# Windowed attention and an ELU layer on one core: queries and keys of batches 1 (second half), 2 and 3 loaded as token blocks and transposed by DMA

## The chip, the core and the metric

The kernel runs on one core of a Trainium2 chip. The metric is the device time of one execution in microseconds; a lower time is better. Engines are named as in the profile: PE is TensorE (PEld its weight load), DVE is VectorE, ACT is ScalarE, POOL is GpSimd and SP is SyncE. SP, ACT and POOL issue DMAs; the data are moved by sixteen DMA engines that all queues share.

## The reference, cut to what matters

```python
# q, k, v: [8 batches, 8 heads, 576 tokens, 64] float32
scores = q @ k.T / 8                      # per batch and head
scores = where(|i - j| <= 32, scores, -1e9)
attn   = softmax(scores)
x      = (attn @ v), heads side by side    # [4608 tokens, 512]
h      = x @ w_in                          # w_in  [512, 2048]
g      = where(h > 0, h, exp(min(h, 0)) - 1)
out    = g @ w_out                         # w_out [2048, 512], out float32
```

The window is narrow: a block of 64 queries needs the 128 keys around it and no others.

## The kernel before

Everything is computed in bf16 with float32 sums. The order of the instructions on every engine is written out by hand; nothing reorders it.

**The layer.** The 4608 tokens are 18 tiles of 256. A tile goes through 8 steps; in each step two blocks of 128 hidden columns are made (`mm1`, L734), ACT takes the exponential (L744), DVE subtracts one (`subtract`, L756; for steps 1, 3 and 4 ACT does it, L754), DVE takes maximum and minimum (`elu`, L767), and two steps later `mm2` adds the product with w_out (L787). There are 144 steps; the first 16 interleave tiles 0 and 1. `elu` of a step runs on DVE at the start of the next one, ahead of the slot "dve".

**Attention beside it.** The queries are 36 pairs of blocks of 64 (`pair i` is blocks 2i and 2i+1; nine blocks are a batch). A table `begin` gives the step at which a pair's `scores` run; from pair 6 on, two pairs begin in one step: pairs 6 and 7 in step 18, 8 and 9 in 26, 10 and 11 in 31, 12 and 13 in 37, then two in every eighth step. One step later comes `mask`, two later `pv` (the product with V), three later `normalize`. The result x must be transposed to xT, [features, tokens], which `mm1` reads: two pairs make a tile. Up to pair 9 TensorE does that (`x_transpose`); from pair 10 on a DMA on SP's queue does (`x_dma`, L455), in steps begin + 3 and begin + 4. Tile 5 is made of pairs 10 and 11, and its first step is step 40.

**Slots.** `at(step, slot, function)` notes work; `run` issues it in the slots "first", "dve" (before `mm1`), "half" (in the middle of it), "mid" (after it) and "end". So where an entry stands decides its place in the queue of its engine, and an engine that waits holds up all that stands behind it.

**Queries and keys.** Scores need qT and kT, [head dimension, tokens], two buffers each for even and odd batches. The data come as float32 with tokens outside. Before the change there are three ways:

- Batches 0 and 1, first half: cast and transposed in pieces at the front.
- Batch 1, second half (`HALF_B`), and batch 2: loaded as float32 on SP (`load_qk`, L132, in pieces of 9 or 18 tokens of one head, 2,304 or 4,608 bytes each), cast to bf16 by ACT or DVE (`cast_qk`, L290, L292), transposed by TensorE in groups of nine (`transpose_qk`, L340) and copied from PSUM by ACT. A one-element DMA, `gate`, holds these loads on SP until the weights are there.
- Batches 3 to 7: loaded and cast in the same way, then written to DRAM by ACT's queue (`write_rows`, L319) and brought back transposed by a DMA on SP (`transpose_rows`, L324).

**V.** `load_v` (L151) loads blocks of 128 tokens of V on POOL's queue, with a cast, into one of three buffers V_e. Blocks with an odd index need V shifted by 64 rows, V_o: it is copied on DVE (`rotate_v`, L175) or by two DMAs on SP (`rotate_v_dma`, L183). `hold_v` is a tiny DVE instruction that makes the loads of a batch wait for a step.

The output rows leave on SP (L803), two stores of 256 KB for a tile.

Of the kernel before, what the change touches and what calls it, by code (L numbers as in the profile page):

```python
# [10 lines left out]
BF16 = mybir.dt.bfloat16  # L11
# [10 lines left out]
def kernel(  # L22
# [9 lines left out]
    nc = tc.nc  # L32

    B, H, S, D = q.shape
# [9 lines left out]
    HP = H // 2  # L44
    NC = 128 // HP
    SJ = S // NC
    VS = 5
# [15 lines left out]
    lpool = ctx.enter_context(tc.tile_pool(name="loads", bufs=2))  # L63
# [53 lines left out]
    HJ = SJ // 2  # L117
    WHOLE, HALF_A, HALF_B = (0, SJ), (0, HJ), (NC * HJ, HJ)
# [4 lines left out]
    def load_qk(b, which, part, engs=(nc.sync, nc.sync)):  # L123
        z, nj = part
        mj = max(nj, HJ)
        t = lpool.tile([128, 2, mj * D], FP32, tag=f"f{which}{mj}",
                       name=f"f{which}", bufs=2 if part is WHOLE else 1)
        qk_f[b, which, z] = t
        src = (q, k)[which][b, :, z:z + NC * nj, :].rearrange(
            "(g h) (c j) d -> c g h (j d)", h=2, j=nj)  # L130
        for h in range(2):
            engs[h].dma_start(out=t[:, h, 0:nj * D], in_=src[:, :, h, :])  # L132
# [4 lines left out]
    def load_cast(b, which, part):  # L137
        z, nj = part
        mj = nj if nj < 3 else HJ + 1
        t = cpool.tile([128, 2, mj * D], BF16, tag=f"c{which}{mj}",  # L140
                       name=f"c{which}")[:, :, 0:nj * D]
        qk_c[b, which, z] = t
        src = (q, k)[which][b, :, z:z + NC * nj, :].rearrange(
            "(g h) (c j) d -> c g h (j d)", h=2, j=nj)
        nc.gpsimd.dma_start(out=t, in_=src)

    def load_v(b, m, rows=(0, 128)):
        lo = 128 * m - WIN
        p0 = max(rows[0], -lo)
        p1 = min(rows[1], S - lo)  # L150
        nc.gpsimd.dma_start(  # L151
            out=V_e[b % 3][p0:p1, m, :, 0:D],
            in_=v[b, :, lo + p0:lo + p1, :].rearrange("h p d -> p h d"))
# [37 lines left out]
    def gate(src, dt=BF16, eng=nc.sync):  # L191
        gates[0] += 1
        t = cpool.tile([1, 1], dt, name=f"gate{gates[0]}")
        eng.dma_start(out=t, in_=src)

    def load_w_in(c, z=0, nz=1):
        w = D_FF // 4 // nz
        c = c * nz + z
        nc.gpsimd.dma_start(
            out=w_in_sb[:, :, c * w:(c + 1) * w],  # L200
            in_=moe_w_in[:, c * w:(c + 1) * w].rearrange(
                "(o p) f -> p o f", p=128))

    def load_w_out(c, z=0, nz=1):
        n = NFO // 4 // nz
        c = c * nz + z
        nc.gpsimd.dma_start(
            out=w_out_sb[:, c * n:(c + 1) * n, :],
            in_=moe_w_out[c * n * 128:(c + 1) * n * 128, :].rearrange(
                "(o p) f -> p o f", p=128))  # L210

    def w_in_at(c):
        return w_in_sb[0:1, 0, (c + 1) * (D_FF // 4) - 1:(c + 1) * (D_FF // 4)]

    for which in range(2):
        load_qk(0, which, HALF_A, (nc.sync, nc.scalar))
# [4 lines left out]
    def edges(i):  # L221
# [24 lines left out]
        out=far, in_=far, compare_op=ALU.is_ge, fill=FAR,  # L246
        base=0, pattern=[[0, 2], [-1, QB]], channel_multiplier=1)
    nc.gpsimd.affine_select(
        out=far, in_=far, compare_op=ALU.is_ge, fill=FAR,
        base=2 * WIN, pattern=[[0, 2], [1, QB]], channel_multiplier=-1)  # L250
    nc.gpsimd.affine_select(
        out=far[:, 0, :], in_=far[:, 0, :], compare_op=ALU.is_ge, fill=FAR,
# [55 lines left out]
    def keys_or_queries(b, which):  # L308
        if which == 0:
            return qT[b % 2].rearrange("p g s -> p (g s)")  # L310
        return kT[b % 2][:, KPAD:KPAD + HP * S]
# [146 lines left out]
    def first_pair(b):  # L458
        return NQB * b // 2
# [27 lines left out]
    for which in range(2):  # L487
        load_cast(0, which, FRONT_B[which])
# [9 lines left out]
    for which in range(2):  # L498
        load_cast(0, which, FRONT_C[which])
# [4 lines left out]
    BOTH = (nc.scalar, nc.vector)  # L504
# [42 lines left out]
    for which in range(2):  # L547
        load_cast(1, which, HALF_A)
# [3 lines left out]
        load_v(1, m)  # L552
    load_w_in(3)
    load_w_out(3)
    for m in range(3, VS):
        load_v(1, m)
    gate(w_in_at(3))
    for which in range(2):
        load_qk(1, which, HALF_B)
    for which in range(2):  # L560
        load_qk(2, which, WHOLE)

# [3 lines left out]
    def at(kk, slot, fn, *args):  # L568
        tasks.setdefault((kk, slot), []).append((fn, args))
# [34 lines left out]
    for which in range(2):  # L604
        at(8 + which, (6, "half")[which], transpose_qk, 1, which, HALF_A, 0,
           HJ, nc.scalar, "s")
        at(14 + which, "mid", cast_qk, 1, which, HALF_B, 0, HJ, BOTH[which])
        at(15 + which, "end", transpose_qk, 1, which, HALF_B, 0, HJ,
           nc.scalar, "s")
    at(6, "dve", edges, 2)  # L610
    at(16, "dve", hold_v, 2)
    for m in range(VS):
        at(16 + m, "mid", load_v, 2, m)
    at(12, "dve", rotate_v, 1, 0, 2)
    for z in range(2):
        at(14 + z, "dve", rotate_v, 1, 2, VS - 1, (z,))

# [4 lines left out]
    for i in range(4, NPAIR):  # L624
        two = i >= FIRST_TWO
        kk, z = begin[i], i % 2 if two else 0
# [5 lines left out]
        n = kk + (3 + z if two else 2)  # L632
# [11 lines left out]
    for b in range(2, B):  # L644
        k0 = begin[first_pair(b)]


        l_qk, l_v, c0 = {2: (0, 0, 0), 3: (15, 24, 22), 4: (35, 36, 41),
                         5: (52, 52, 57), 6: (68, 68, 73),
                         7: (84, 84, 89)}[b]  # L650
        if b >= 3:
            at(l_qk, "end", load_qk, b, 0, WHOLE)
            at(l_qk, "end", load_qk, b, 1, WHOLE)
            if b > 3:
                at(l_v, "dve", hold_v, b)
            for m in range(VS):
                at(l_v + m, "mid", load_v, b, m)
        if b <= 3:

            if b == 2:  # L660
                at(k0, "dve", rotate_v, b, 0, 1)
            at((21, 28)[b - 2], "mid", rotate_v_dma, b, 3 - b)
        else:
            for n, back in enumerate((10, 8, 3, 2)):
                m0 = 2 * (n // 2)
                at(k0 - back, "dve", rotate_v, b, m0, m0 + 2, (n % 2,))
        if b == 2:

            for n, (which, j0) in enumerate(((0, 0), (0, 9), (1, 0), (1, 9))):
                at((18, 20, 21, 23)[n], ("mid", "end", "end", "mid")[n],  # L670
                   cast_qk, b, which, WHOLE, j0, 9,
                   (nc.vector, nc.scalar, nc.scalar, nc.vector)[n])
                at(22 + n, "end" if n == 1 else "mid", transpose_qk, b, which, WHOLE, j0, 9,
                   nc.scalar, "su"[n % 2])
            continue


        free = [f for f in range(c0, k0) if f not in starts]
        for n, (which, j0) in enumerate(
                (which, j0) for which in range(2) for j0 in (0, 6, 12)):  # L680
            at(free[n], "end", cast_qk, b, which, WHOLE, j0, 6,
               nc.vector if free[n] < 26 else nc.scalar)
            if j0 == 12:
                at(free[n], "end", write_rows, b, which)
                at(free[n] + (3 if free[n] == 29 else 4), "mid",
                   transpose_rows, b, which)

# [50 lines left out]
    def exponents(kk, z):  # L740
        ps = psH[kk][z]
        e_sb = mpool.tile([128, ps.shape[1], TT], FP32, tag="e_sb",
                          name="e_sb")
        nc.scalar.activation(e_sb, ps, AX.Exp)  # L744
        e_t[kk, z] = e_sb
        if kk > 0:
            subtract(kk, z)

    def subtract(kk, z):
        e_sb = e_t.pop((kk, z))  # L750
        m_sb = mpool.tile([128, e_sb.shape[1], TT], BF16, tag="m_sb",
                          name="m_sb")
        if kk in (1, 3, 4):
            nc.scalar.activation(m_sb, e_sb, AX.Copy, bias=-1.0)  # L754
        else:
            nc.vector.tensor_scalar(m_sb, e_sb, -1.0, None, ALU.add)  # L756
        m_t[kk, z] = m_sb

    def elu(kk, z=0):
        if z == 0:  # L760
            g_t[kk] = mpool.tile([128, FG, TT], BF16, tag="g_sb", name="g_sb",
                                   bufs=8)
        if kk == 0:
            subtract(kk, z)
        ps = psH[kk][z]
        w = ps.shape[1]
        nc.vector.scalar_tensor_tensor(  # L767
            g_t[kk][:, z * w:(z + 1) * w, :], ps, 0.0, m_t.pop((kk, z)),
            ALU.max, ALU.min)
# [119 lines left out]
```

## Time and profile before

| | |
|---|---|
| median of 3 runs | 302.76 us (302.54 to 302.93) |
| the profiled execution | 302.52 us, its span 300.8 us |
| PE busy, transposes L340 included | 291.8 us, 97% |
| DVE, ACT, POOL busy | 240.9, 170.2, 52.7 us |
| transposes of q and k, L340 | 72, of them 54 between 43 and 93 us (4.0 us busy) |
| queue q1 (SP): packets, MB | 47330, 35.61 |
| queue q0 (POOL): packets, MB | 44976, 10.10 |
| first product of steps 18, 26, 31, 37, 40 | 51.96, 69.92, 80.66, 92.57, 99.19 us |

The times in the profile count from the start of the span; 1.7 us of the execution lie around it. Busy shares are averages over the whole span. A DMA row has the issue time on its queue and, apart from it, the time to landing. q0 is the queue of POOL, q1 that of SP, q10 that of ACT. A packet is one piece of one transfer; its size is counted at the destination, so a row of 64 elements is 128 bytes.

### The profile page before, as it was taken

Reading aid. Unit: us, or ns where it says so; the run is one execution under the profiler, and the core shown is the slowest. Engines: PE = TensorE matmul, PEld = TensorE weight load, DVE = VectorE, ACT = ScalarE, POOL = GpSimd, SP = SyncE. Lnnn points to the kernel's source line nnn. Section 1 sums busy time; section 2 is a strip of 40 time slices with the busy share of each in tenths; the row PEclk is TensorE's granted clock in tenths of the full one; section 3 lists DMA queues with packets and bytes.
Section 4 is the critical chain, followed back from the end, with each engine's and each line's share of the span. In section 5 each row is a group of like instructions: output and inputs, shape, how many; then the busy total and the mean of one; then the engine's idle time right before and its main releaser. Section 6 shows DMA issues by size and latency. Waiting matters only on the chain.

```text
span 300.8 us, 7664 instructions
## 1 busy us (share of the span) xinstructions
PE 291.8 (97%) x3066; PEld 198.6 (66%) x3118; DVE 240.9 (80%) x479; ACT 170.2 (57%) x258; POOL 52.7 (18%) x74
## 2 busy tenths in 40 slices
PE   7899999999999999999999999999999999999995
PEld 3585567677666666666666666666666666666673
DVE  7788588978787988888889789887988787877773
ACT  3783648688655567456745665467535353534342
POOL 8777203520005000410032002300000000000000
PEclk9999999999999999999999999999999999999999
DMA  9999999999957978999899989997921111111011
GB/s 190 168 200 203 185 233 349 370 179 231 241 159 199 239 116 270 244 267 135 161 256 323 172 203 252 312 153 137 268 54 72 35 72 38 70 37 70 2 70 71
DMA packets 94070, 52.68 MB, mean 175 GB/s; under 512 B 78163, under 2 KB 83795, under 8 KB 94035
## 3 DMA queue, kind: packets, MB, share of 16 engines
q1 hardware_dynamic: 47330, 35.61, 44.7%
q0 software_dynamic: 44976, 10.10, 44.2%
q10 hardware_dynamic: 1728, 6.49, 6.3%
q8 instruction: 24, 0.39, 0.6%
q14 instruction: 12, 0.09, 0.1%
HBM read 36.70 MB, written 15.34 MB: 173 GB/s over the span
## 4 chain that ended last, share of the span: by engine, by line
PE 85%; DMA 5%; issue 3%; DVE 2%; ACT 2%; POOL 2%; POOLq 0%; ACTq 0%; DVEq 0%
PE ps L734 39%; PE psY L787 38%; PE psS L416 4%; DMA out_dram<-y_sb 3%; PE psS L384 3%; DMA c<-in_k_dram 2%; ACT e_sb L744 1%; DVE g_sb L767 1%; PE ptx L335 1%; PE psXT L438 1%; POOL Vo L158 1%; DVE qkb L292 0%; ACT qkb L290 0%; PE ptx L340 0%; PE psS L364 0%
## 5 line engine op out<-in xcount | busy, mean ns | idle before, releaser
L744 ACT ACTIVATE e_sb<-ps 128x512 f32<-128x512 f32 (+1 forms) x145 | 86.3, 596 | 113.4 <-PE ps L734 106.0
L734 PE MATMUL ps<-xT,w_in_sb 128*128 128x256 bf16 (+1 forms) x1168 | 149.7, 271 | 0.1
L787 PE MATMUL psY<-w_out_sb,g_sb 128*128 128x512 bf16 (+2 forms) x541 | 139.3, 373 | 2.9 <-issue 0.3
L734 PEld LDWEIGHTS <-w_in_sb 128*128 128x128 bf16 x1168 | 110.4, 98 | 36.8 <-issue 0.8
L767 DVE SCALAR_TENSOR_TENSOR g_sb<-ps,m_sb 128x512 bf16<-128x512 f32 (+1 forms) x145 | 99.3, 686 | 13.1 <-DVE m_sb L756 0.5
L756 DVE TENSOR_SCALAR m_sb<-e_sb 128x512 bf16<-128x512 f32 (+1 forms) x142 | 61.5, 433 | 34.3 <-ACT e_sb L744 32.3
L787 PEld LDWEIGHTS <-g_sb 128*128 128x128 bf16 x592 | 55.9, 98 | 38.7
L151 POOL DMA_DIRECT2D Ve<-in_v_dram x37 | 32.5, 892 | 132.8 <-PE psS L416 79.5
L395 ACT ACTIVATE pu<-psS 128x1024 bf16<-128x1024 f32 x36 | 36.6, 1023 | 0.9 <-PE psS L384 0.8
L428 DVE TENSOR_TENSOR x_st<-psS,rc 128x512 bf16<-128x512 f32 x36 | 24.9, 692 | 1.2
L290 ACT CAST qkb<-f 128x768 bf16<-128x768 f32 (+1 forms) x29 | 25.0, 862 | 0.0
L404 DVE TENSOR_TENSOR pm<-pu,masks 128x1024 bf16<-128x1024 bf16 x32 | 21.8, 682 | 0.0
L416 PEld LDWEIGHTS <-pm 128*64 128x64 bf16 x512 | 9.6, 110 | 7.3 <-DVE pm L404 6.5
L292 DVE COPY y_sb<-psY 128x512 f32<-128x512 f32 (+1 forms) x18 | 12.2, 676 | 1.5 <-PE psY L787 1.5
L384 PEld LDWEIGHTS <-kT 64*128 64x128 bf16 x560 | 9.4, 95 | 4.6 <-issue 4.4
L290 ACT COPY y_sb<-psY 128x512 f32<-128x512 f32 (+1 forms) x19 | 10.8, 569 | 2.5 <-PE psY L787 2.5
L384 PE MATMUL psS<-qT,kT 64*128 64x64 bf16 x560 | 11.8, 191 | 0.1
L416 PE MATMUL psS<-Ve,pm 128*64 128x65 bf16 x288 | 11.5, 196 | 0.1
L290 ACT COPY qT<-ptx 128x1152 bf16<-128x1152 bf16 (+4 forms) x9 | 7.7, 882 | 5.0 <-PE ptx L340 3.5
L416 PE MATMUL psS<-Vo,pm 128*64 128x65 bf16 x224 | 10.3, 196 | 0.0
L175 DVE COPY Vo<-Ve 64x1040 bf16<-64x1040 bf16 (+1 forms) x22 | 9.1, 413 | 0.7
L425 DVE RECIPROCAL rc<-psS 128x8 f32<-128x8 f32 x36 | 7.2, 199 | 0.9 <-PE psS L416 0.9
(54 smaller groups left out, 91.3 us busy)
## 6 DMA issues: line engine op xcount, KB each, us to landing
out_dram<-y_sb SPq DMA_DIRECT2D x36, 256.0 KB, 3.5
f<-in_q_dram SPq DMA_DIRECT2D x12, 576.0 KB, 6.3
f<-in_k_dram SPq DMA_DIRECT2D x12, 576.0 KB, 8.0
in_dram<-qkb ACTq DMA_DIRECT2D x10, 576.0 KB, 4.2
Ve<-in_v_dram POOLq DMA_DIRECT2D x21, 128.0 KB, 12.6
w_out_sb<-in_moe_w_out_dram POOLq DMA_DIRECT2D x3, 512.0 KB, 10.4
Ve<-in_v_dram POOLq DMA_DIRECT2D x14, 96.0 KB, 11.6
w_in_sb<-in_moe_w_in_dram POOLq DMA_DIRECT2D x2, 512.0 KB, 10.4
```

The costliest lines, as they stand in the source:

```text
L151: nc.gpsimd.dma_start(out=V_e[b % 3][p0:p1, m, :, 0:D], in_=v[b, :, lo + p0:lo + p1, :].rearrange("h p d -> p h d"))
L290: nc.scalar.copy(d_, s_)
L384: nc.tensor.matmul(psS[:, h % 2, hp * 128 + z * QB:hp * 128 + (z + 1) * QB], lhsT=keys, rhs=qT[b % 2][base:base + 64, hp, QB * qb:QB * (qb ...
L395: nc.scalar.activation(pu, _bap(psS, [psS.ap[0], [1, 1024]]), AX.Exp, scale=SCALE)
L404: nc.vector.tensor_mul(pm, pu, _bap(mm, [mm.ap[0], [0, H], [1, 2 * QB]]))
L416: nc.tensor.matmul(psS[QB * z:QB * (z + 1), par, hp * VD:(hp + 1) * VD], lhsT=pm[:, par * HP + hp, z * QB:(z + 1) * QB], rhs=vv[:, qb // 2 ...
L428: nc.vector.tensor_mul(x_st, _bap(psS, [psS.ap[0], [VD, HP], [512, 2], [1, D]]), _bap(rc, [rc.ap[0], [2, HP], [1, 2], [0, D]]))
L734: nc.tensor.matmul(o, lhsT=w_in_sb[:, do, fo * 128:(fo + 1) * 128], rhs=r, start=(do == 0), stop=(do == NDO - 1))
L744: nc.scalar.activation(e_sb, ps, AX.Exp)
L756: nc.vector.tensor_scalar(m_sb, e_sb, -1.0, None, ALU.add)
L767: nc.vector.scalar_tensor_tensor(g_t[kk][:, z * w:(z + 1) * w, :], ps, 0.0, m_t.pop((kk, z)), ALU.max, ALU.min)
L787: nc.tensor.matmul(sum_of(t, ts, c), lhsT=g_t[n][:, j, ts * 128:(ts + 1) * 128], rhs=w_out_sb[:, s * FG + j, cols_of(c)], start=(s == 0 an ...
```

## The change

Queries and keys of the second half of batch 1, of batch 2 and of batch 3 take a new way. `load_tokens` loads a block of up to 128 tokens of all heads on POOL's queue, with the cast, into a bf16 tile [tokens, 512], in runs of 64 elements. `transpose_tokens` is a DMA on SP that writes the block transposed into qT or kT. Batch 1 has six blocks of 96 tokens, batches 2 and 3 ten each (four of 128 and one of 64, for q and for k). The blocks of batch 1 are put on POOL's queue after the last weights and ahead of the last two V blocks of batch 1; those of batch 2 follow, then V of batch 2, the blocks of batch 3 and V of batch 3. The casts, TensorE's transposes and the copies from PSUM of these parts go, and so do batch 3's way through DRAM, the gate, the early `hold_v` and one of the two buffers for float32 loads. `rotate_v` of batch 1 moves from steps 14 and 15 to 17 and 18, `rotate_v_dma` of batches 2 and 3 from steps 21 and 28 to 23 and 33. In the odd steps from 17 to 31 the subtraction goes from DVE to ACT.

```diff
-                       name=f"f{which}", bufs=2 if part is WHOLE else 1)
+                       name=f"f{which}", bufs=1)
...
+    def load_tokens(b, which, s0, n):
+        tag = f"tok{which}{s0}" + ("h" if b == 1 else "")
+        t = lpool.tile([128, H * D], BF16, tag=tag, name="tok", bufs=1)
+        tokens[b, which, s0] = t, n
+        nc.gpsimd.dma_start(
+            out=t[0:n].rearrange("p (h d) -> p h d", h=H),
+            in_=(q, k)[which][b, :, s0:s0 + n, :].rearrange("h p d -> p h d"))
+
+    def transpose_tokens(b, which, s0):
+        t, n = tokens.pop((b, which, s0))
+        nc.sync.dma_start_transpose(
+            out=keys_or_queries(b, which).rearrange(
+                "x (g s) -> x g s", g=HP)[:, :, s0:s0 + n],
+            in_=t[0:n])
...
+    REST = [(s0, 96) for s0 in range(NC * HJ, S, 96)]
+    BLOCKS = [(s0, min(128, S - s0)) for s0 in range(0, S, 128)]
+    rest = [(which, *blk) for blk in REST for which in range(2)]
+    blocks = sorted(((which, *blk) for blk in BLOCKS for which in range(2)),
+                    key=lambda x: (x[1] - x[0] * 129, x[0]))
+    for x in rest:
+        load_tokens(1, *x)
     for m in range(3, VS):
         load_v(1, m)
-    gate(w_in_at(3))
-    for which in range(2):
-        load_qk(1, which, HALF_B)
-    for which in range(2):
-        load_qk(2, which, WHOLE)
+    for x in blocks:
+        load_tokens(2, *x)
...
-        at(14 + which, "mid", cast_qk, 1, which, HALF_B, 0, HJ, BOTH[which])
-        at(15 + which, "end", transpose_qk, 1, which, HALF_B, 0, HJ,
-           nc.scalar, "s")
...
-    at(16, "dve", hold_v, 2)
     for m in range(VS):
-        at(16 + m, "mid", load_v, 2, m)
+        at(12, "mid", load_v, 2, m)
     at(12, "dve", rotate_v, 1, 0, 2)
     for z in range(2):
-        at(14 + z, "dve", rotate_v, 1, 2, VS - 1, (z,))
+        at(17 + z, "dve", rotate_v, 1, 2, VS - 1, (z,))
+    for which, s0, n in rest:
+        at(14, "end", transpose_tokens, 1, which, s0)
+    for which, s0, n in blocks:
+        at(18, "end", transpose_tokens, 2, which, s0)
+        at(19, "mid", load_tokens, 3, which, s0, n)
+        at(30, "mid", transpose_tokens, 3, which, s0)
+    for m in range(VS):
+        at(20, "mid", load_v, 3, m)
...
-            at((21, 28)[b - 2], "mid", rotate_v_dma, b, 3 - b)
+            at((23, 33)[b - 2], "mid", rotate_v_dma, b, 3 - b)
...
-        if kk in (1, 3, 4):
+        if kk in (1, 3, 4) or kk in range(17, 32, 2):
             nc.scalar.activation(m_sb, e_sb, AX.Copy, bias=-1.0)
```

The loads, casts, groups of transposes and the way through DRAM of batches 2 and 3 go from the loop over batches, which now begins these at batch 4.

## The prediction

> **What bounds the kernel now.** I read the page's busy shares first, then its slices, then the groups of instructions and the timeline between 43 and 110 us, where the change acts, and last the DMA queues window by window.
>
> ```profile
> PE 291.8 (97%) x3066; PEld 198.6 (66%) x3118; DVE 240.9 (80%) x479; ACT 170.2 (57%) x258; POOL 52.7 (18%) x74
> ...
> DMA  9999999999957978999899989997921111111011
> ```
>
> TensorE is busy 97% of the span, so time comes off only where TensorE gets less work, and goes on wherever it must wait. The DMA row is the warning: from the start to about 83 us the sixteen DMA engines are full, and from 90 to 218 us (slices of 7.5 us) they are at seven tenths or more. The timeline of TensorE shows what a step costs (one line for each step's first product):
>
> ```profile
> 65.41 1.04 PE L734 MATMUL ps<-xT,w_in_sb 128*128 128x256 bf16 x8
> 66.28 0.67 PE L340 MATMUL ptx<-ident,qkb 128*128 128x128 bf16 x9
> ...
> 67.68 1.03 PE L734 MATMUL ps<-xT,w_in_sb 128*128 128x256 bf16 x8
> ...
> 72.35 1.04 PE L734 MATMUL ps<-xT,w_in_sb 128*128 128x256 bf16 x8
> ...
> 74.09 1.04 PE L734 MATMUL ps<-xT,w_in_sb 128*128 128x256 bf16 x8
> ```
>
> Step 24 (65.41) lasts 2.27 us, with nine transposes in it; step 27 (72.35), with nothing extra, 1.74. So nine transposes are worth about 0.5 us of the path, less than their 0.67 busy, since they are pipelined.
>
> **What the skill says.** "DMA: Bandwidth & Descriptors", "Queues, rings and completion order": each engine takes turns between the queue rows that have work, packet by packet. The trace agrees, and gives the price, in three windows (an x transpose beside V loads; V loads alone, twice):
>
> ```profile
> q1 hardware_dynamic: 764, 0.20, 84.2%
> q0 software_dynamic: 762, 0.10, 78.3%
> ...
> q0 software_dynamic: 2355, 0.30, 232.7%
> ...
> q0 software_dynamic: 6620, 0.83, 387.0%
> ```
>
> In 133 to 135 us both queues move the same number of packets, 382 per us each. In 102 to 104 the V rows alone move 1178 per us, in 63 to 70 only 946; I take 1050. Together the two queues make 763, not 1050: a transpose packet costs the rows more than its own time. The same page, "SWDGE vs HWDGE vs iDMA", says that a casting DMA must be issued from GpSimd; here every cast load (V, weights, c) is indeed on q0, so all new loads join q0. "Advanced Engine Details and Errata", "X-Bar Transpose (TRN2)", says transpose DMAs are as fast as regular ones. Alone that is near: two x transposes are 1,024 packets of 256 B at 19 ns (16.1% of 16 engines over 8 us); beside q0 it doesn't hold.
>
> **The change part by part.**
>
> *Removed from TensorE:* six groups of nine transposes (L340), two in steps 15 and 16, four in 22 to 25: 6 x 0.5 = 3.0 us off the path, 1.0 before step 18 and 3.0 by step 26.
>
> *ACT and DVE.* Casts and evictions go: on ACT 5 casts at about 1.0 and 6 copies at 1.23 us (12.5 us between 43 and 93), on DVE 3 of batches 1 and 2 and the 4 of batch 3, about 4.5. Eight subtractions (odd steps 17 to 31) move from DVE (0.43 each) to ACT (0.63 each, the three of L754): ACT gains 5.0, DVE loses 3.5. Both end with less to do; I cost this at nothing: TensorE hides it, and from 52 to 71 us, where they were busiest, DVE worked 16.05 of 19 us and ACT 14.81, both more than they will. Were that cover gone, the eight longer instructions would cost 8 x 0.2 = 1.6 us at most. Also nothing: the cut of f from two buffers to one, since batch b's last cast (step 48 for batch 4) precedes the next load (step 52); the loss of one gate and of batch 3's two row writes and two 18-tile transposes, whose queues have the new work instead.
>
> *Moved to q0.* A token block of 128 rows x 8 heads is the form of a V load: 1,024 packets, 0.89 us of POOL to issue. Half batch 1 has 4,608 row packets, batches 2 and 3 have 9,216 each. Before them the f loads moved the same data in 4,608-byte pieces on SP. GpSimd's queue keeps order, so V of batch 1 (1,792 packets after the tokens), batch 2 and batch 3 (4,608 each) stand behind them: 34,048 packets in all. At most eight are in flight; the ninth V load waited until the first had landed:
>
> ```profile
> 49.66 7.47 POOL L151 DMA_DIRECT2D Ve<-in_v_dram  x8 [16.76 <-DVE Ve L170]
> ...
> 64.00 0.88 POOL L151 DMA_DIRECT2D Ve<-in_v_dram  x1 [6.87 <-DMA Ve<-in_v_dram]
> ```
>
> *Added to SP:* 26 transposes (6 of 96 rows, 20 of batches 2 and 3). No row shows one from a token tile; the nearest is xT<-x_st, 1.2 us of SP to issue, 2.6 us to landing, 512 packets per 128 rows, so 11,520 packets. Bounds: 14 ns per packet and engine (row rate, no loss in mixing, a gain for me) to 27 ns (16/382 - 16/1050 us); I take the measured mix.
>
> *The clock of q0.* The last weights (issued at 28.8, 12.7 us to landing) end at about 41.
>
> - To V of batch 1: 2,304 packets beside transposes at 382 take 6.0 us, the other 4,096 at 1050 take 3.9: 51. The first token lands at 42, each further one 1.4 us later (384 packets mixed, 384 alone), so the fourth transpose is issued at 46.2 and lands 2.6 later at 49; the scores of pairs 6 and 7 need it at 51.9 (step 18, 52.9 less 1.0). Hidden; V rotations of steps 17 and 18 wait under 1 us.
> - To the second V block of batch 2, 11,008 packets: 4,608 beside transposes 12.1 us, 512 beside the four output stores at 160 per us 3.2, the rest 5.6: 72. DVE wants it for the rotation of step 26 at about 69 (72.0 before, less 3.0). DVE waits some 3 us, and TensorE some 2 at step 28, for elu stands behind it. All of V of batch 2: 74.6.
> - To all V of batch 3, 13,824 packets: 12.1 beside transposes, 1.6 beside stores, 8.5 alone, and 0.7 for the V copy of batch 2: 97.5.
>
> *The path that sets the end.* At step 33 SP holds rotate_v_dma of batch 3, which now waits for those V blocks until 97.5. Behind it in SP's order stand the stores of tile 3 and the x transposes of pairs 10 and 11:
>
> ```profile
> 87.05 1.46 SPq L803 DMA_DIRECT2D out_dram<-y_sb  x2
> 89.08 3.28 SPq L455 DMA_TRANSPOSE xT<-x_st  x2
> 92.40 1.27 SPq L132 DMA_DIRECT2D f<-in_q_dram  x2
> ```
>
> From 97.5: two copies (1.1 us to issue), two stores (0.7), two transposes (2.4), the last landing about 2 later, as 1 MB of copies and stores at some 340 GB/s goes ahead: 103.7. Step 40 needs this xT. It began at 99.19; with 3.0 off it could begin at 96.2, and begins at 103.7: **4.5 us later than before**. The earlier waits lie inside this one. After it TensorE has no slack to catch up. Batch 4's loads are issued at 103 and not 92.4, but steps are shifted too; I leave that at 0, up to +2 for casts that wait.
>
> Sum: the profiled execution took 302.52 (span 300.8 and 1.7 outside); + 4.5 = 307.0. The median of the three runs is 0.24 higher: **307.3**.
>
> **The rivals.**
>
> *A. q0 keeps up (faster).* If mixed queues lose nothing, 45,568 packets at 1150 take 39.6 us and the stores 5.5: V of batch 3 lands at 86, SP is free before the 88 at which x_st of pair 11 is ready, the V of batch 2 is there at 66. Then only TensorE's 3.0 count: 299.7. The point that decides is V of batch 3 landing before 90. For it: 1178 per us was seen. Against: the 382 each in the mix, and again 777 and 836 packets in 195 to 197 us, that is about 400 each.
>
> *B. A draw.* V of batch 3 lands at 92 to 93.5; x of pair 11 at 98.5 to 99.5; TensorE's saving is given back within 0.6 us: 302.8.
>
> *C. Worse.* Rows at 946 all the way (V of batch 3 at 99.5), and batch 4's casts wait 2 us more for f on ACT: 311. If scores waited for whole tiles and not for blocks, step 26 would wait for batch 2's last transpose at 72 and step 37 for batch 3's at 95; both lie before the wait of step 40 and change nothing.
>
> *D. That the change does not do what it says* (transposes still on TensorE) is excluded by the diff: no transpose_qk remains for these parts.
>
> **How the numbers follow.** Likeliest, with C: 0.75, its own range 304 to 311. A: 0.20. B: 0.05. Measurement tells 0.2% (0.6 us) from no change. The range 299.5 to 311.5 reaches into A, since without it a quarter would be left out. Faster 0.20, same 0.05, slower 0.75.
>
> **What would show it.** Right: 18 transposes left in L340; SP's rotate copy of batch 3 issued at 95 to 100 us; x transposes of pairs 10 and 11 only after it; a gap of TensorE before the first product of step 40, released by a DMA xT<-x_st; a smaller one near step 28 behind DVE's rotation. Wrong: the copy issued before 90, no gap there, and q0 at over 500 packets per us beside transposes.

## The result, and the profile after

The changed kernel takes **316.69 us** (median of 6 runs, 315.46 to 318.47); the kernel before, run beside it, 302.57. The ratio is 1.0477, 95% interval [1.044, 1.0514]: 14 us slower, where 4.5 were forecast. The profiled execution took 318.47 us, its span is 316.7; it is the slowest of the six, so the account below has to explain 16 us and not 14. Medians here and below are of all runs, while ratios leave out slow runs, those over 1.5% above the fastest of their kernel, so that the two do not match for e12.

The page first: busy shares, then three rows of the forty slices (7.9 us each).

```profile
PE 297.2 (94%) x3064; PEld 197.0 (62%) x3064; DVE 235.5 (74%) x463; ACT 164.1 (52%) x255; POOL 72.6 (23%) x100
...
PE   7999996998995579999999999999999999999995
...
PEclk9999999799998959999999999999999999999999
DMA  9999999999999992799989998999852111111011
```

TensorE has holes from 48 to 55, 71 to 79 and 95 to 119 us where it had none before. Behind that nothing differs: every step from 42 on lasts what it did. The PEclk row shows a second thing, a granted clock that falls in the slices from 55, from 95 and from 111 us, during waits or right behind them. The DMA engines are now full until 119 us; before, they had gaps from 83 us on.

The saving is there: the first products of steps 24 and 25 in TensorE's timeline, with no transposes between them any more, lie 1.74 us apart where they lay 2.27:

```profile
68.12 1.04 PE L751 MATMUL ps<-xT,w_in_sb 128*128 128x256 bf16 x8
...
69.86 1.04 PE L751 MATMUL ps<-xT,w_in_sb 128*128 128x256 bf16 x8
```

The table of waits for TensorE (total, times, longest) and its timeline name the holes:

```profile
PE psS L403 <- DMA kT<-tok: 7.5, 3, 3.2
PE ps L751 <- DMA xT<-x_st: 5.5, 1, 5.5
```

```profile
55.08 0.41 PE L403 MATMUL psS<-qT,kT 64*128 64x64 bf16 x16 [2.85 <-DMA kT<-tok]
...
72.56 0.44 PE L403 MATMUL psS<-qT,kT 64*128 64x64 bf16 x18
74.50 0.38 PE L403 MATMUL psS<-qT,kT 64*128 64x64 bf16 x14 [1.50 <-DMA kT<-tok]
...
97.10 0.55 PE L403 MATMUL psS<-qT,kT 64*128 64x64 bf16 x26
100.82 0.34 PE L403 MATMUL psS<-qT,kT 64*128 64x64 bf16 x6 [3.17 <-DMA kT<-tok]
...
113.01 1.86 PE L751 MATMUL ps<-xT,w_in_sb 128*128 128x256 bf16 x8 [5.52 <-DMA xT<-x_st]
```

Three times (steps 18, 26, 37) the scores wait in the middle of a pair for keys, each time for one block: kT 384 of batch 1 (landed at 55.03), then kT 512 of batches 2 and 3 (74.45 and 100.78). The fourth wait is the one that was forecast, step 40 for its xT. SP's own queue shows how that one came about:

```profile
94.25 2.48 SPq L161 DMA_TRANSPOSE qT<-tok  x2
100.60 1.55 SPq L202 DMA_DIRECT2D Vo<-Ve  x2
102.26 2.57 SPq L820 DMA_DIRECT2D out_dram<-y_sb  x2
104.93 3.30 SPq L474 DMA_TRANSPOSE xT<-x_st  x2
```

After the last transpose of batch 3, SP stands still until V of batch 3 is there (its last block landed at 101.67), then issues the copies, the stores and only then the x transposes, the last of which lands at 112.87. Step 40 starts at 113.01, 13.8 us later than before (99.19). The rest is clock: in the windows of steps 19, 40 and 41 it is 0.57, 0.50 and 0.79. The columns are the length of the window, busy time of the `mm1` products and of their weight loads, granted clock, DMA share and GB/s.

```profile
56.70:59.71 3.01, 1.92 (x9) 1.16 (x8) 0.57 1.32 312
...
113.01:116.38 3.37, 1.87 (x9) 1.14 (x10) 0.50 0.99 399
116.38:118.57 2.19, 1.49 (x8) 1.02 (x8) 0.79 1.65 348
```

Steps 40 and 41 together last 5.56 us where they took 3.49: 2.1 us. So 13.8 + 2.1 = 15.9 us, the difference of the spans (316.7 and 300.8).

### The profile page after: what moved, and what is told of

Its sections match the earlier page's. It is cut to its first block, busy times and chain, and to the rows that moved or that the text cites. A ratio compares the mean times of both kernels' runs of the same rounds, so it can differ in the third digit from the quotient of the medians.

```text
span 316.7 us, 7647 instructions
## 1 busy us (share of the span) xinstructions
PE 297.2 (94%) x3064; PEld 197.0 (62%) x3064; DVE 235.5 (74%) x463; ACT 164.1 (52%) x255; POOL 72.6 (23%) x100
## 4 chain that ended last, share of the span: by engine, by line
PE 77%; DMA 9%; SPq 5%; DVE 4%; POOL 1%; issue 1%; ACT 1%; POOLq 0%; DVEq 0%; ACTq 0%
PE ps L751 35%; PE psY L804 34%; DMA kT<-tok 5%; SPq L161 5%; PE psS L435 3%; PE psS L403 3%; DMA c<-in_k_dram 2%; DMA xT<-x_st 2%; DVE g_sb L784 1%; DVE m_sb L773 1%; ACT e_sb L761 1%; PE ptx L354 1%; PE psXT L457 1%; POOL Vo L177 1%; DVE pm L423 0%
## 5 line engine op out<-in xcount | busy, mean ns | idle before, releaser
L751 PE MATMUL ps<-xT,w_in_sb 128*128 128x256 bf16 (+1 forms) x1168 | 152.4, 274 | 5.5 <-DMA xT<-x_st 5.5
L804 PE MATMUL psY<-w_out_sb,g_sb 128*128 128x512 bf16 (+2 forms) x592 | 150.1, 379 | 0.0
L751 PEld LDWEIGHTS <-w_in_sb 128*128 128x128 bf16 x1168 | 111.9, 99 | 45.0 <-DMA xT<-x_st 5.6
L773 DVE TENSOR_SCALAR m_sb<-e_sb 128x512 bf16<-128x512 f32 (+1 forms) x134 | 58.9, 440 | 38.1 <-ACT e_sb L761 36.0
L804 PEld LDWEIGHTS <-g_sb 128*128 128x128 bf16 x592 | 56.5, 99 | 40.0 <-issue 1.7
L170 POOL DMA_DIRECT2D Ve<-in_v_dram x37 | 31.0, 848 | 117.6 <-PE psS L435 92.7
L309 ACT CAST qkb<-f 128x768 bf16<-128x768 f32 x24 | 19.8, 827 | 0.0
L155 POOL DMA_DIRECT2D tok<-in_k_dram x13 | 11.0, 846 | 6.0 <-DMA Ve<-in_v_dram 3.5
L155 POOL DMA_DIRECT2D tok<-in_q_dram x13 | 10.8, 828 | 5.5 <-DMA Ve<-in_v_dram 2.1
```

The source lines that it names most:

```text
L155: nc.gpsimd.dma_start(out=t[0:n].rearrange("p (h d) -> p h d", h=H), in_=(q, k)[which][b, :, s0:s0 + n, :].rearrange("h p d -> p h d"))
L170: nc.gpsimd.dma_start(out=V_e[b % 3][p0:p1, m, :, 0:D], in_=v[b, :, lo + p0:lo + p1, :].rearrange("h p d -> p h d"))
L309: nc.scalar.copy(d_, s_)
L751: nc.tensor.matmul(o, lhsT=w_in_sb[:, do, fo * 128:(fo + 1) * 128], rhs=r, start=(do == 0), stop=(do == NDO - 1))
L804: nc.tensor.matmul(sum_of(t, ts, c), lhsT=g_t[n][:, j, ts * 128:(ts + 1) * 128], rhs=w_out_sb[:, s * FG + j, cols_of(c)], start=(s == 0 an ...
```

## The experiments

Each is a whole kernel; times are medians, with the ratio to the kernel before on the same chip. "T" stands for the DMA transposes of a batch, "rows" for its token loads.

**Which wait sets the end?** First the block that steps 26 and 37 wait for, loaded and transposed ahead of the others.

```diff
-                    key=lambda x: (x[1] - x[0] * 129, x[0]))
+                    key=lambda x: (-200 if x == (1, 512, 64) else
+                                   x[1] - x[0] * 129, x[0]))
```

> Only the order of the blocks of batches 2 and 3 differs: the last key block (tokens 512 to 575) comes first and not eighth. Theory (a key read reaches over the edge): the first query block of a batch reads 32 key columns ahead of its own, and in head pairs 1 to 3 these belong to the last key block of the head pair before; so the scores at steps 26 and 37 wait for that block. Then the waits of TensorE for kT<-tok at steps 26 (1.7 us more than before) and 37 (4.2 us more) vanish, only the one at step 18 (3 us) stays. The x transposes of pairs 10 and 11 still land at 111 to 113 us, since the queues carry the same data, so step 40 waits longer and the total falls by 0 to 2 us: 314.5 to 317. Rival (the transposes as a whole are late, any block): the waits at 26 and 37 stay within 1 us of what they are.

Measured 317.25 us (1.0499 [1.0451, 1.0546]). Both waits are gone (2.42 us each for steps 26 and 37, as without a wait), and the total is the same: all of it turned into the next wait, which grew from 5.5 us to 13.2:

```profile
PE ps L752 <- DMA xT<-x_st: 13.2, 1, 13.2
```

That confirms where these two waits came from. The first query block of a batch also reads the 32 columns ahead of its own; for head pairs 1 to 3 they lie in the last key block of the pair before, so the scores of the first pair of blocks need block 512 at once. It also shows that those waits are covered by the later one.

Then that later wait: V's copy for batch 3 moved on SP behind the x transposes, without (e2) and with (e3) the order of e1.

```diff
-            at((23, 33)[b - 2], "mid", rotate_v_dma, b, 3 - b)
+            at((23, 35)[b - 2], ("mid", "end")[b - 2], rotate_v_dma, b, 3 - b)
```

> Only the V copy of batch 3 on SP moves, from ahead of the stores of tile 3 and the x transposes of pairs 10 and 11 to behind them. Theory (SP's order): the x transposes no longer wait for V of batch 3; the wait of step 40 (5.6 us, plus some 1.6 of slow clock after it) goes, the one of step 37 (4.2) stays: 308 to 311 us. Rival (the x transposes are late because the queues are full): they are issued at once after step 34 but still land at 108 or later, and the total stays at 314 to 317.

> Both changes of order. Theory: waits of steps 26, 37 and 40 gone, what stays is the wait of step 18 (3.3 us and 1.3 of slow clock after it) less the 3.0 of transposes saved: 303 to 306 us. Rival (full queues set the date of everything): what goes at 37 and 40 comes back at the next reader of batch 3's V or of x, and it stays above 309.

Measured 313.43 (1.0362 [1.0337, 1.0386]) and 313.94 us (1.0392 [1.0347, 1.0437]): 3 us are back, not the 6 to 14 that I expected. The x transposes are issued at 96.0 and 95.1 only, for SP is busy with T of batch 3 until 94 to 95, and they take 8 to 10 us to land. Step 40 starts at 106.5 and 106.4. The order on SP is a part of the cause; the next runs ask whether full queues are the rest.

**Is it the amount in the queues, or the depth of the backlog?** In e5 GpSimd reads the token or V tile three loads back before it issues the next one, so that at most four row loads are in flight.

```diff
+        flight[0].append(ap)
+        if len(flight[0]) >= 4:
+            nc.gpsimd.tensor_copy(seen, flight[0].pop(0))
```

> The changed kernel with one thing more: from the first token block to V of batch 3, POOL reads one element of the row load three back before it issues the next, so that at most four row loads are in flight and not eight. The data moved and every order stay. Theory (backlog): a transpose lands late because many row loads are queued on each DMA engine; with four in flight the transposes land in 4 to 6 us and not in 8.3, the waits at steps 18, 26, 37 and 40 shrink by a third to a half: 308 to 313 us. Rival (amount): the number of packets sets the dates, not the backlog; V of batch 3 lands at the same 102 us or later, and the total is 315 to 320.

Measured 319.86 us (1.0585 [1.0565, 1.0604]), slower still. T of batch 1 lands sooner and the wait at step 18 is gone (2.49 us), but V of batch 3 lands at 103.4 and step 40 starts at 114.6. A shallow backlog mends the first date and does nothing good for the last. So the amount was taken away instead: batch 3's transposes (e9) or batch 3's rows (e10; its transposes read batch 2's tokens), each kernel leaving out that part of the data.

```diff
-        at(30, "mid", transpose_tokens, 3, which, s0)
```

> The full change without the ten DMA transposes of batch 3; its rows are loaded, but its scores read what batch 1 left in qT and kT (this part of the result is left out). Theory (amount in the window 41 to 102 us): 4,608 transpose packets less, at 27 ns each on one of sixteen engines 7.8 us of queue time; V of batch 3 lands at 93 to 95 and not at 102, SP is free earlier, no wait at step 37, the wait of step 40 shrinks to 0 to 3 us: 306 to 310 us. Rival (only the rows count): V of batch 3 lands at 99 or later and the total is over 311.

```diff
+        if b == 2:
+            tokens[3, which, s0] = t, n
...
-        at(19, "mid", load_tokens, 3, which, s0, n)
```

> The full change without the ten row loads of batch 3; its transposes run, but read the token tiles of batch 2 (this part of the result is left out). Theory (amount): 9,216 row packets less, at 14 ns 8.1 us of queue time; V of batch 3 lands at 90 to 94, no wait at step 37, that of step 40 0 to 3 us: 306 to 310 us, within 2 us of the kernel without the transposes. Rival (the transposes and their place on SP's queue count, not the rows): over 312.

Measured 306.64 (1.0155 [1.0126, 1.0184]) and 309.2 us (1.0267 [1.0222, 1.0312]). V of batch 3 lands at 90.8 and 82.4 instead of 101.7, and neither kernel waits at steps 37 to 40. What they still lose are the waits of steps 18 and 26 (4.5 us for keys in e9, 5.5 in e10) and slow clock behind them. SP's queue in e9:

```profile
90.68 1.11 SPq L202 DMA_DIRECT2D Vo<-Ve  x2
91.88 1.98 SPq L819 DMA_DIRECT2D out_dram<-y_sb  x2
93.97 3.27 SPq L474 DMA_TRANSPOSE xT<-x_st  x2
```

The same order, ten microseconds earlier, and the x transposes are in time. In e10 SP's own issuing sets the date of the copy: it issues batch 3's ten transposes from 78 to 92.6, and the copy at 92.8. The 4,608 transpose packets that e9 lacks bring V forward by 10.9 us, 423 per us; close to the 409 per us that each queue gets in the mix in the changed kernel, from 62 to 64 us:

```profile
q1 hardware_dynamic: 818, 0.19, 83.1%
q0 software_dynamic: 817, 0.10, 80.8%
```

From 77 to 79 us only rows move, as fast as they did before, 1,175 per us:

```profile
q0 software_dynamic: 2350, 0.30, 249.9%
```

**Why does the path after V take 11.2 us and not 6.2?** The V loads of batch 4 are let go at step 41 instead of 36.

```diff
-            l_qk, l_v, c0 = {4: (35, 36, 41), 5: (52, 52, 57),
+            l_qk, l_v, c0 = {4: (35, 41, 41), 5: (52, 52, 57),
```

> The full change, but the five V loads of batch 4 are held to step 41 and not 36, so that none is in flight when V of batch 3 has landed and SP issues the copy, the stores and the x transposes of pairs 10 and 11. It asks what makes that path 11.2 us long and not the 6.2 of the forecast. Theory: the rows of V of batch 4 beside it. Then from the landing of V of batch 3 to the last x transpose it takes 6 to 8 us, step 40 starts at 108 to 110, total 311 to 314 us. Rival: the copies and stores alone make it: the path stays 10 us or longer and the total 315 to 318 us.

Measured 312.54 us (1.0344 [1.0289, 1.0399]), as the theory had it. SP's queue in it (in this execution the steps from 15 to 37 begin 3 to 4 us later than in the changed kernel, so it is the length of the path that counts, not its dates):

```profile
101.17 2.00 SPq L202 DMA_DIRECT2D Vo<-Ve  x2
103.28 1.36 SPq L820 DMA_DIRECT2D out_dram<-y_sb  x2
104.74 2.67 SPq L474 DMA_TRANSPOSE xT<-x_st  x2
```

V of batch 3 lands at 102.56, 0.9 us later than in the changed kernel, but the last x transpose lands at 109.80: 7.2 us after it. In the changed kernel V of batch 4 is issued from 96.6 on and fills q0. The V copies, issued at 100.6 and 101.7, hardly move beside it; from 101 to 104 us:

```profile
q0 software_dynamic: 2868, 0.36, 429.6%
q1 hardware_dynamic: 14, 0.00, 0.7%
```

They take 8 us to land instead of 3.3 to 3.5. Of the 5.0 us that my path was short, V of batch 4 makes 4.0.

The same question was asked of the kernel before, in its quiet part: 24 spare row loads beside x transposes.

```diff
+    for step, deep, n in ((107, 7, 14), (115, 1, 2), (122, 2, 8)):
+        at(step, "dve", hold_spare)
+        for i in range(n):
+            at(step, "mid", load_spare, i % deep, 128 * (i % 4))
```

> The kernel before, with 24 row loads of the token form added into spare tiles in its quiet last part, held to three steps: 14 with up to 7 in flight (x transposes of steps 109, 110 beside them), 2 with one in flight (steps 117, 118), 8 with two in flight (steps 122 on, x of 125, 126). The price in question is the time from the issue of a transpose to its landing, 2.4 us there without loads. Theory (depth): many row loads in flight hold a transpose back beyond the sharing of packets: 6 to 9 us at 7 in flight, 4 to 6 at two, 3 to 4 at one. Rival (only turns by packet): 512 packets at about 400 per us make 1.3 us in place of 0.5, so 3.2 to 3.8 us in all three. The output is not touched, the total moves by under 1 us.

One run, 309.29 us, of which 7 are the instrument's own (DVE's hold waited for spare loads still in flight). What it can say is the landing time of an x transpose: 2.45 us alone, 2.94 and 2.98 with two row loads in flight, 6.28 and 7.06 with up to seven. At seven that is what the theory of depth said; at two it is below what either side had expected. The case of one load left no clean reading.

**Why is step 18 late?** In e13 GpSimd reads qT and kT of batch 1 before it issues the first rows of batch 2.

```diff
+            nc.gpsimd.tensor_copy(seen, d[0:1, S - 1:S])
...
+    at(15, "first", after_rest)
+    for x in blocks:
+        at(15, "first", load_tokens, 2, *x)
```

> The full change, but the token rows of batch 2, and with them all that stands behind on POOL's queue, are held until the transposes of batch 1 have landed (a one-element read of qT and of kT by GpSimd at step 15). It asks what makes the transposes of batch 1 land 7.4 to 9.2 us after their issue. Theory: the rows of batch 2 queued beside them. Then the transposes of batch 1 land 3 to 6 us after issue, the wait at step 18 (3.3 us) is gone, and since the rows begin about 5 us later, V of batch 3 lands about 5 us later too and step 40 starts at 115 to 118: 318 to 322 us. Rival: the transposes themselves are this slow or are kept up by the f loads: they still take 7 us or more, and step 18 lasts 5 us or longer.

Measured 320.29 us (1.0577 [1.0517, 1.0637]). T of batch 1 lands 2.3 to 5.8 us after issue (7.4 to 9.2 in the changed kernel), and the scores of step 18 run through:

```profile
52.37 0.64 PE L403 MATMUL psS<-qT,kT 64*128 64x64 bf16 x32
```

All else is later by the time that the rows were held: step 26 waits 8.1 us, V of batch 3 lands at 105.5, step 40 starts at 114.7. So the rows queued beside the transposes made step 18 late, and mending that alone loses.

**What does each batch cost by itself?** These kernels are the kernel before with one batch loaded in the new way, or two. Batch 3 alone (e7):

```diff
+    for which, s0, n in blocks:
+        at(20, "mid", load_tokens, 3, which, s0, n)
+        at(30, "mid", transpose_tokens, 3, which, s0)
...
-        if b >= 3:
+        if b >= 4:
```

> Only batch 3 takes the new way; TensorE's work is that of the kernel before, ACT and DVE lose the six casts of batch 3, DRAM two writes and two 18-tile transposes. Theory (amount): token rows of batch 3 follow V of batch 2 from 50 us on and are done by 75 to 80, in time; V of batch 3 lands at 85 to 88, the copy ahead of the x transposes is issued in time or up to 2 us late: 302.4 to 304.5. Rival (the form itself is slow, any 20 transposes beside rows wait 8 us): waits at steps 37 and 40 as in the full change, 308 to 314.

Batch 2 alone (e6):

```diff
-    for which in range(2):
-        load_qk(2, which, WHOLE)
+    for x in blocks:
+        load_tokens(2, *x)
...
+    for which, s0, n in blocks:
+        at(18, "end", transpose_tokens, 2, which, s0)
```

> Only batch 2 takes the new way; batches 1 and 3 as in the kernel before, the subtraction stays on DVE. TensorE loses 36 transposes, 2.0 us. Theory (amount of row packets beside large loads): the float32 loads of batches 1 and 3 (4,608-byte packets, one for one with rows) hold the token rows to some 80 per us until about 52 us; the last key block of batch 2 lands at 72 to 76 us, wait at step 26 of 3 to 6 us, V of batch 3 early enough, no wait at 37 and 40: 304 to 308 us. Rival (backlog of all three batches needed): without batches 1 and 3 the queue drains in time and 2.0 us are gained: 300.4 to 301.5.

Batches 1 and 2, which is the changed kernel with batch 3 as it was (e8):

```diff
-        at(19, "mid", load_tokens, 3, which, s0, n)
-        at(30, "mid", transpose_tokens, 3, which, s0)
...
-        if b >= 4:
+        if b >= 3:
```

> The full change but for batch 3, which goes the old way (float32 loads on SP at step 15, casts, DRAM). TensorE loses all 54 transposes, 3.0 us. Theory: the wait of step 18 stays (3 us), the one of step 26 grows to 4 to 8 as batch 3's large loads stand beside the tokens of batch 2, those of steps 37 and 40 go since V of batch 3 is early: 305 to 310 us. Rival (batch 3's rows cause all of it): 300 to 303.

Batch 1 alone (e15):

```diff
+    for x in rest:
+        load_tokens(1, *x)
...
-        load_qk(1, which, HALF_B)
...
+    for which, s0, n in rest:
+        at(14, "end", transpose_tokens, 1, which, s0)
```

> Only the second half of batch 1 goes the new way; batches 2 and 3 are loaded, cast and transposed as before, with the subtraction on DVE. It asks what batch 1's part costs alone. Theory: on SP's queue the transposes of batch 1 stand behind the f loads of batch 2, 2.4 MB, and land at 53 to 56 us, so step 18 waits 3 to 5 us, which nothing later gives back: 304 to 307 us. Rival: batch 1 lands in time, and TensorE's eighteen transposes less give 1.0 us: 301.5 us.

Batch 3 alone costs nothing that matters, 302.92 us (1.003 [1.0013, 1.0048]): its rows land by 71.5 and its V by 75.6, its transposes 2.4 to 5.7 us after issue, nothing waits. It saves nothing either, for its way never used TensorE. The others missed what I expected: batch 2 alone 313.52 (1.0374 [1.0338, 1.0411]), batches 1 and 2 319.37 (1.0566 [1.0511, 1.0621]), batch 1 alone 311.09 us (1.0297 [1.025, 1.0343]). With batch 2 alone step 15 lasts 4.9 us and step 26 10.6, where TensorE waits 7.0 us for keys. With batch 1 alone I had the mechanism and not its size: T of batch 1 stands on SP behind 2.4 MB of float32 loads and lands as late as 60.76, so step 18 waits twice and lasts 10.23 us.

```profile
50.91 0.29 PE L401 MATMUL psS<-qT,kT 64*128 64x64 bf16 x8
54.60 0.40 PE L401 MATMUL psS<-qT,kT 64*128 64x64 bf16 x8 [3.40 <-DMA kT<-tok]
57.95 0.61 PE L401 MATMUL psS<-qT,kT 64*128 64x64 bf16 x16 [2.95 <-DMA kT<-tok]
```

With batches 1 and 2, ACT stood still for 12.65 us at step 26, for batch 3's rows, still on the old way, are written to DRAM by ACT's queue, and that instruction waited for a transpose on SP's (last section). Mended versions of batch 2 alone followed. In e12 its rows are held until the float32 loads of batch 1 have landed, and then come in the order in which they are needed, block 512 of the keys first:

```diff
+            nc.gpsimd.tensor_copy(
+                seen, qk_f[1, which, HALF_B[0]][0:1, 1, 0:1])
...
+        at(12, "mid", load_tokens, 2, *x)
+        for m in {3: (0, 1), 7: (2, 3, 4)}.get(n, ()):
+            at(12, "mid", load_v, 2, m)
```

> Only batch 2 goes the new way, as in the kernel with batch 2 alone, with three changes of order: the last key block first, the row loads only after the loads of batch 1's second half have landed, and V blocks 0, 1 after four token blocks, 2 to 4 after eight. Theory (amount and due dates, there is room for one batch): no wait at step 15; the four blocks due at step 26 land at 64 to 68 us, before it; 2.0 us of TensorE's work are saved: 300.2 to 302 us. Rival (eight loads in flight beside transposes are too slow for any order): a wait of 2 to 6 us at step 26, 304 to 308 us.

In e16, moreover, SP issues batch 3's two writes, and V's last three blocks come behind all tokens:

```diff
-        nc.scalar.dma_start(
+        (nc.sync if b == 3 else nc.scalar).dma_start(
...
-        for m in {3: (0, 1), 7: (2, 3, 4)}.get(n, ()):
+        for m in {3: (0, 1), 9: (2, 3, 4)}.get(n, ()):
```

> As in the run with batch 2 alone in due order, but the two writes of batch 3's rows to DRAM are issued by SP and not by ACT, and V blocks 2 to 4 of batch 2 come after its last tokens. It asks whether ACT, held at the issue of such a write until a transpose on SP's queue has landed, is what delays steps 26 and 37. Theory: ACT is no longer held, step 26 lasts under 3 us, the wait at step 37 shrinks: 301 to 305 us. Rival: the rows of batch 2 land too late in any case: step 26 still lasts over 4 us and the total is 308 us or more.

Measured 311.36 (1.0224 [1.0204, 1.0244]; six runs from 308.20 to 317.98) and 314.38 us (1.04 [1.0366, 1.0433]): both missed. ACT's timeline in e12, of an execution of 312.93 us, has the hold once more, 4.51 us until a transpose of kT had landed:

```profile
69.44 0.63 ACTq L336 DMA_DIRECT2D in_dram<-qkb  x1
70.17 0.60 ACT L778 ACTIVATE e_sb<-ps 128x512 f32<-128x512 f32 x1 [4.51 <-DMA kT<-tok]
```

In e16 it is gone and step 26 lasts 2.96 us, as expected, although two edits share that. But the write of batch 3's keys now stands on SP behind the V copies of batch 2, and these behind V itself, which lands at 87.86:

```profile
85.28 3.06 SPq L200 DMA_DIRECT2D Vo<-Ve  x2
88.44 3.57 SPq L341 DMA_TRANSPOSE qT<-in_dram  x1
92.11 0.61 SPq L336 DMA_DIRECT2D in_dram<-qkb  x1
96.17 5.14 SPq L341 DMA_TRANSPOSE kT<-in_dram  x1
```

The transpose of these keys is issued at 96.17 and step 37 lasts 14.18 us. What ACT does not wait for, SP does.

**ACT's share.** The subtraction of the odd steps back on DVE:

```diff
-        if kk in (1, 3, 4) or kk in range(17, 32, 2):
+        if kk in (1, 3, 4):
```

> The full change with the subtraction of the odd steps 17 to 31 back on DVE. Theory: ACT's eight subtractions are hidden behind the waits for DMA, 316 to 318 us, no difference. Rival (the 12.8 us that elu waits for ACT's result are a cost): 310 to 314 us.

Measured 316.58 us (1.0487 [1.0462, 1.0511]): no difference to the changed kernel.

No version beats the kernel before; the nearest, batch 3 alone, is level with it.

## Why the prediction was right in direction and a third of the size

The measured time lies 5.2 us above the upper end of the range.

**Right.** The direction, and the mechanism of the last wait: V of batch 3 late on q0, SP standing at its copy, the x transposes behind it, step 40 waiting for them. TensorE's saving is 2.9 us (3.0 forecast): steps 15, 16, 18 and 22 to 25 give 1.0, 0.1 and 1.8 apart from their waits. ACT and DVE at nothing holds (e11). Rival C's remark that waits for late keys at steps 26 and 37 would lie inside that of step 40 holds as well (e1). The price of mixing, 382 packets per us for each queue, was 409 here.

**Wrong, the sum of the last path.** Its mechanism held; what failed is its size. Against 307.0 for a profiled execution, 318.47 is 11.5 more. Three terms of the path make 11.3 of it:

| term | forecast | measured |
|---|---|---|
| V of batch 3 lands | 97.5 us | 101.67 us, +4.2 |
| from there to the last x transpose | 6.2 us | 11.2 us, +5.0 |
| steps 40 and 41 after the wait | 3.49 us | 5.56 us, +2.1 |

*"97.5"* was mis-sized by 7%: from 41 us, 60.7 and not 56.5; 2.1 us of the 4.2 had come by the end of V of batch 2 (76.7 for 74.6). I charged packets at the rates of full queues. That the amount sets this date is shown (e9, e10). Where the 4.2 us went is not shown; holes in the traffic of all queues (last section) come to about as much, 2.1 us up to 76.7 and 2.3 from there on (counted in steps of 0.1 us).

*"6.2"* took SP's issue times and the copies' bandwidth, but not what else would be in the queues by then: V of batch 4. It costs 4.0 (e14), and my sum does not have it at all; the 0 to +2 that I left for batch 4 was for its float32 loads and casts.

*The clock* was not in the sum. The Trainium skill's "TensorE: Matmul & The Clock Gate", "What's actually happening", says that an idle window of about 3.4 us puts TensorE at half clock and that busy time brings it back. The trace agrees on the half (0.50 in step 40, after a wait of 5.5 us). The page's figure is no safe limit for a wait, though: the clock was halved around the end of shorter ones too, of 2.85 us here and of 2.1 us at step 26 of e10, but not after 2.5 us at step 18 of e10. In all these traces a stretch at half clock, the one at a kernel's very end apart, lasts 3.41 us or a multiple of it (3.41, 3.41 and 6.83 here). A forecast of a wait should have carried that price.

**Wrong, the step "Hidden" at step 18.** I let a transpose land 2.6 us after issue, as x transposes do, and put the fourth at 49. It was issued in time, at 46.99, and landed at 55.03, for seven or eight row loads stood beside it. The group views of L161, all 26 new transposes, and of L455, the x transposes of the kernel before:

```profile
DMA to landing us min/median/max: 6.5/8.3/11.1
...
DMA to landing us min/median/max: 2.4/2.6/9.3
```

I had taken the rate of the mixed queues from the trace and its latency from a place where nothing was mixed, though the trace before had this price too. Its x transpose of 100.58 us landed 7.1 us later, beside V loads; and in the window from 102 to 104, which I read as V loads alone, that transpose was waiting, while q1 moved 6 packets. This error did not set the end (without the wait at step 18, e5 and e13 end no earlier), nor did the next one (e1).

**Wrong, steps 26 to 28.** I expected DVE to wait for V of batch 2 and TensorE at step 28. Instead step 26, which began 1.7 us later than before, waited for a key block that I had thought was needed last; the columns ahead of a batch's first block had escaped me. V's second block landed at 70.56 (72 forecast), ahead of that step.

**Rivals A and B** (queues keep up, a draw) are excluded: V of batch 3 landed at 101.67, not before 90 (A) or at 92 to 93.5 (B).

## What to carry to other kernels

Work taken from an engine at 97% is worth only what the new way's transfers leave of it: count the packets that join each queue, and follow them to the last instruction that stands behind them in program order. Price a transfer in the state of the queues in which it will run, latency and rate both, with the loads of the next stage that will have started by then. Taking away an early wait in such a chain, or spreading its load, moves the delay to a later one (e1, e5, e13, e16). Less traffic ahead of the late transfer or beside it gave 4 to 10 us (e9, e10, e14), a better order on SP 3 us (e2). And waits of 2.9 to 5.5 us on TensorE cost up to 2.1 us more in clock here.

## What the runs showed of the hardware that I had not expected

- Queue latency, not transpose speed: the same kind of transpose lands in 2.45 us alone, 2.9 to 3.0 beside two row loads of 128 KB, 6.3 to 7.1 beside up to seven, and 8.3 (median) here.
- Two queues whose packets are both under way get turns that are even in packets: 818 against 817 in two microseconds, most of them of 256 B on one and of 128 B on the other. The Trainium skill's "DMA: Bandwidth & Descriptors", "Queues, rings and completion order", gives a packet as some 9 to 17 descriptors; the equal counts show that rows and transposes get equally many in a turn, not how many that is.
- A transfer that SP issues while row loads are queued does not get such turns at once: the V copies issued at 100.6 moved their first packets at 105.1, and q0 moved 2,868 packets against 14 of q1 from 101 to 104. In the kernel before, the first packets of the x transpose issued at 100.58 moved at 104.4. Why is open.
- An instruction that issues a DMA on ACT's queue can wait for a transfer of SP's queue with which it shares no data (4.5 us in e12, 12.65 in e8). In the traces the completions of both queues count on the same few semaphores, taken in turn. ACT's last wait before the write in e8 is for semaphore 117, on which SP's transpose landed at 78.97 and on which the write then counts; ACT issued the write at 79.05. In e12 it is semaphore 116, at 69.36 and 69.44. That e16, where SP issues the write, has no such wait on ACT fits this.
- Holes in all queues that I can't explain: from about 90.3 us on, for over a microsecond, the DMA engines moved 31 GB/s and less with rows and transposes waiting (each figure of the first row is 37.5 ns, from 90 us on). Another stands at 99.3 to 100.3, just before V of batch 3 landed (second row, 0.25 us each, from 92 us on):

```profile
GB/s 154 154 143 147 143 143 133 61 31 31 31 27 31 31 20 20 14 10 10 10 7 10 10 0 10 10 3 10 7 10 10 10 10 3 10 7 10 10 10 10
...
GB/s 149 151 143 114 100 135 122 108 31 151 144 157 160 158 160 147 155 160 159 158 154 151 162 142 220 168 128 137 116 54 19 18 19 139 169 158 103 100 101 146
```

Stretches of 0.3 us or more under 60 GB/s come to 4.4 us between 41 and 102 us. Holes in which packets of 256 B or less take over 0.6 us each stand in the kernel before as well, at 105.7 to 106.6 for one, with V rows, stores and an x transpose waiting, and in every experiment. In all of them a DMA transpose was in flight, and no trace has one ahead of its first DMA transpose (42.0 us here, 75.7 in the kernel before), though the queues are full there. That the transposes cause them is not shown, and neither is that the 4.4 us are the 4.2 by which V of batch 3 was late: no run takes the holes away.
